# Values by key block with 128 columns of weights, and logits by blocks of 128 tokens, in a fused attention and mixture-of-experts kernel

## The chip, the core and the metric

The kernel runs on one core of a Trainium2 chip. The metric is the device time of one launch in microseconds. TensorE (PE in the profile) is the matmul engine; its weight loads are shown apart, as PEld. VectorE is DVE, ScalarE is ACT, GpSimd is POOL, and SyncE (SP) mostly issues DMAs.

## The reference

Eight batches with eight heads, 576 positions and 64 features a head, attend over a sliding window of 64 positions. Each of the 4608 tokens then goes to one of eight experts, the one with the highest logit.

```python
scores = scale * np.matmul(q, k.transpose(0, 1, 3, 2))
mask = (rel >= 0) & (rel < 64)                   # rel = query position - key position
attn = softmax(np.where(mask, scores, -1e9))
x = np.matmul(attn, v)                           # to rows of 512 = 8 heads x 64, one a token
logits = normalized(x) @ normalized(expert_emb).T / tau
e = argmax(logits)
out = gate * (relu(x @ w1[e]) @ w2[e])           # w1: 512 x 1024, w2: 1024 x 512
```

## The kernel before

**Tiling of the attention.** The tokens are cut into 36 blocks T of 128, each of two half blocks of 64: half z = 0 is key and query block 2T, half z = 1 is block 2T + 1. A batch has nine such 64-blocks, so batches begin at the 64-blocks 0, 9, 18 and so on; in eight of the 36 values of T one of the halves begins a batch and has no previous block. The window is as long as a 64-block, so a query sees its own block's keys up to itself and the previous block's keys behind that, 64 in all. The kernel keeps one score for each of the 64 places and notes by a mask which block it belongs to.

Heads lie in pairs: the partitions hold two heads hp of 64 features (or 64 keys) each, and u counts four such pairs. A matmul for one head, one half and one u therefore uses a 64x64 quarter of the 128x128 array, and four quarters (two hp, two z) can be at work at once. The profile writes this shape as 64\*64, rows by columns of the array that an instruction uses. A matmul of plain f32 operands that is written once in the program stands twice in the profile, as two weight loads and two matmuls; transposes and the experts' matmuls stand once.

**A step of the attention.** The loop `stages(s)` writes out one step for each block, a software pipeline over several blocks. In the order of PE's instructions:

- `scores(s)`, L215: 16 matmuls of 64\*64, 128 keys moving (64 where a batch begins)
- `logits(s - 4)`, L329: for each of four chunks c of 128 features and for each half of 64 tokens, a matmul with 64 columns of weights (the turned x, 128 features by 64 tokens) and 8 moving columns (the experts' embeddings), 128\*64 in the profile
- `attn_transposes(s - 1)`, L245, into `back`: four transposes of 128\*128
- `x_transposes(s - 3)`, L314, into `xback`: four transposes of 128\*128
- at times `ranks`, L366 and L367: two small bf16 matmuls
- `values(s - 2)`, L276: 32 matmuls of 64\*64 with 65 moving columns (64 features and a column of ones, for the softmax's sum), into the PSUM pair of banks `pair`

The other engines work beside it. ACT copies the own-block scores (L222), DVE puts the previous block's over them (`all_scores`, L225) and takes maxima (L229), POOL subtracts them (`less_max`, L233), ACT takes exponentials (L236). After the transposes ACT copies the turned weights into `aM[:, 0]` (L255); DVE writes `aM[:, 1]`, the weights times one mask (`attn_prev`, L258), and POOL multiplies `aM[:, 0]` by the other mask (`attn_own`, L261). DVE divides `pair` by the sums into rows of x (`x_out`, L297 to L299). POOL sends finished rows to their expert's place in DRAM by indirect DMAs (`place`, L412).

`values` takes the two masks in two passes. The first pass multiplies the weights that belong to the previous block (`aM[:, 1]`) with that block's values, the second those of the own block (`aM[:, 0]`, which POOL finishes last) with the own block's. Both pile up in `pair`. In each pass a half z meets another block of values, so z = 0 and z = 1 need matmuls of their own.

**After the loop.** The last blocks' steps are written out by hand and woven with the first expert slot's layer 1 (`layer1`, L827, fp32r operands, 128\*128, 256 moving columns). Then follow the counts and ranks of the tokens, the loads of the chosen experts' weights, and 20 slots of expert work (L827 and L887), which take the rest of the time.

Of the kernel before, what the change touches and what calls it, by code (L numbers as in the profile page):

```python
# [21 lines left out]
P = 128  # L22
B, H, S, D = 8, 8, 576, 64
N, DM, DF, E = 4608, 512, 1024, 8
WIN = 64
NB = S // WIN
# [29 lines left out]
K_ID, K_OWN, K_PREV, K_SEL, K_E, K_DESC, K_P, K_F, K_SL, K_U = 0, 128, 256, 384, 448, 456, 464, 465, 473, 476  # L56
# [3 lines left out]
def constants():  # L60
    c = np.zeros((P, K_W), np.float32)
    p = np.arange(P)
    c[:, K_ID:K_ID + P] = np.eye(P)

    r, col = (p % WIN)[:, None], (p % WIN)[None, :]
    c[:, K_OWN:K_OWN + P] = r <= col
    c[:, K_PREV:K_PREV + P] = r > col
    c[:, K_SEL:K_SEL + WIN] = col[:, :WIN] > r
    c[:, K_U:K_U + P] = p[:, None] < p[None, :]
    c[:, K_E:K_E + E] = np.arange(E) * N  # L70
    c[:, K_DESC:K_DESC + E] = E - np.arange(E)
    c[:, K_P] = p
    c[:, K_F:K_F + E] = (p[:, None] % 32) == np.arange(E)

    for a, (g, j) in POS.items():
        c[a, K_SL:K_SL + 3] = KIND[:g].count(KIND[g]), KIND[g] == "H", P * j
    t = np.full((P, NT + 1), OOB, np.int32)
    t[:, :NT] = np.arange(NT)[None, :] * P + p[:, None]
    return c, t
# [3 lines left out]
def attention_moe(ctx, tc, q, k, v, emb, tau, w1, w2, kc, kt, out):  # L83
    nc = tc.nc
# [46 lines left out]
    pair = psp.tile([P, 2, 512], F32, name="pair")  # L131
# [12 lines left out]
    embT = ap.tile([P, 4, 32], F32, name="embT", bufs=1)  # L144
# [37 lines left out]
    def vblock(g):  # L182
        return vb[:, g // 2 % RV, g % 2]

    sm, st = {}, {}
    sides = [(hp, z) for hp in range(2) for z in range(2)]
# [78 lines left out]
    def values(T):  # L265

        px[T] = pair
        m = aM.pop(T)
        o, p = m[:, 0], m[:, 1]
        for h, start in ((p, True), (o, False)):  # L270
            for u in range(4):
                for hp, z in sides:
                    g, pr, pz = 2 * T + z, slice(64 * hp, 64 * hp + 64), slice(64 * z, 64 * z + 64)
                    if start and g % NB == 0:
                        continue
                    nc.tensor.matmul(pair[pz, hp, u * (D + 1):(u + 1) * (D + 1)], lhsT=h[pr, u, pz],  # L276
                                     rhs=vblock(g - start)[pr, u], start=u == 0 and (start or g % NB == 0),
                                     stop=not start and u == 3)

    xr = {}  # L280
    NXR = 10
# [41 lines left out]
    def logits(T):  # L323
        G = OF[T]
        o2 = plv[:, G % 2, T - GROUPS[G][0]]
        t = xT.pop(T)
        for c in range(4):
            for o in (0, 64):
                nc.tensor.matmul(o2[o:o + 64], lhsT=t[:, c, o:o + 64], rhs=embT[:, c, :E],  # L329
                                 start=(c == 0), stop=(c == 3))  # L330

    def in_rows(G):

# [121 lines left out]
    for i, s0 in enumerate((8, 10, 15, 18, 21, 24, 26, 28)):  # L455
        c, h = divmod(i, 2)
# [3 lines left out]
    for i, s0 in enumerate((29, 30, 30, 31, 31, 32, 32, 33)):  # L460
        c, h = divmod(i, 2)
# [8 lines left out]
    def stages(s):  # L470
# [18 lines left out]
        if there(4):  # L489
            logits(s - 4)  # L490
# [12 lines left out]
        if there(2):  # L503
            values(s - 2)
# [176 lines left out]
    xb, xt, xp, ph, hp, po = {}, {}, {}, {}, {}, {}  # L681
# [344 lines left out]
    T, G = NT - 1, len(GROUPS) - 1  # L1026
# [16 lines left out]
    tokens(T - 2)  # L1043
    layer1(0, 0)
    logits(T - 4)
    own_scores(T)
    split_hi(0, w2raw, w2h)
# [5 lines left out]
    psm2 = ctx.enter_context(tc.tile_pool(name="psm2", bufs=1, space=PSUM, reuse_waits="tile"))  # L1053
    more = [psm2.tile([P, 512], F32, name=f"ph{i}") for i in (2, 3)]
    values(T - 2)
    maxima(T)
    xT_evac(T - 3)
# [8 lines left out]
    attn_halves(T - 1)  # L1066
    layer1(0, 2)
    logits(T - 3)
    ranks(G - 2)
    sum_counts(CUTS[1])  # L1070
# [11 lines left out]
    hidden_lo(0, 0)  # L1082
    x_transposes(T - 2, back)
    values(T - 1)
    xT_evac(T - 2)
    squares(T - 2)
# [112 lines left out]
def laid_out(inputs):  # L1199

    q, k, v = (np.asarray(inputs[n]).reshape(B, 4, 2, S, D) for n in "qkv")
    qt, kt = (x.transpose(2, 4, 1, 0, 3).reshape(P, 4, NT, P).transpose(2, 0, 1, 3).reshape(NT, P, 4 * P) for x in (q, k))
    vt = np.ones((2, WIN, B * NB, 4, D + 1), v.dtype)
    vt[..., :D] = v.reshape(B, 4, 2, NB, WIN, D).transpose(2, 4, 0, 3, 1, 5).reshape(2, WIN, B * NB, 4, D)
    vt = vt.reshape(P, NT, 2, 4, D + 1).transpose(1, 0, 2, 3, 4)

    col = np.arange(DM)
    feature = (col // D % 4 * 2 + col // (4 * D)) * D + col % D
    place = (col % P // 32) * P + col // P * 32 + col % 32
    c, t = constants()  # L1210
    given = {"q": qt, "k": kt, "v": vt, "emb": inputs["moe_expert_emb"][:, feature],
             "tau": np.reshape(inputs["moe_tau"], (1, 1)), "w1": inputs["moe_w1"][:, feature[place]],
             "w2": inputs["moe_w2"], "kc": c, "kt": t}
    return {n: np.ascontiguousarray(a) for n, a in given.items()}
# [16 lines left out]
```

## Time and profile before

| What | Value |
|---|---|
| time, median of 3 runs | 627.56 us (627.01 to 629.45) |
| the profiled execution: its own time | 626.38 us |
| its span, first to last instruction | 624.6 us |
| granted TensorE clock, mean | 0.994 |
| PE busy, of the span | 593.9 us, 95% |
| matmuls of `values` (L276) | 2176 in the profile |
| matmuls of `logits` (L329) | 576 in the profile |

The profile shows one execution. A row of a timeline has the start in us from the span's start, the time from the first start to the last end of the merged instructions, the engine, the line, the operation with its tiles (out<-in), the shape on the array, the size of the moving operand and the count. Matmuls are pipelined and their ends are modelled, so the distance from start to start tells more than the length of one.

### The profile page before, as it was taken

To read this page: it belongs to the slowest core of one execution; us is meant where nothing else is said; L and a number is where in the kernel's file an instruction comes from. 1 tells how busy PE (TensorE), PEld (TensorE's weight loads), DVE (VectorE), ACT (ScalarE), POOL (GpSimd) and SP (SyncE) were. 2 spreads that over 40 slices of the span, in tenths; PEclk is the share of its full clock that TensorE was granted. 3 is DMA by queue.
4 is the path that set the end of the run, shared out by engine and by line. 5 is a ranking of instruction groups with operands and counts; after the bars stand their busy time and mean duration, and the time that the engine had idled before them with its cause. 6 is when DMAs were issued, how large, how long until landed. Compare 5 with 4: busy or idle time off the path is not lost.

```text
span 624.6 us, 18570 instructions
## 1 busy us (share of the span) xinstructions
PE 593.9 (95%) x7210; PEld 531.1 (85%) x7210; DVE 426.0 (68%) x882; ACT 354.1 (57%) x559; POOL 241.6 (39%) x270
## 2 busy tenths in 40 slices
PE   8899989887898799999999999999999999999995
PEld 7787878776788699889988999899889998998884
DVE  2878888888677657676666776657666677657622
ACT  2666776766541346565466665646676476636533
POOL 2668888888732133213104431142023331222011
PEclk9999999999999999999999999999999999999998
DMA  8877888886334588877786897848788877775341
GB/s 302 266 218 252 272 257 268 268 252 196 143 111 184 134 274 259 267 216 253 234 277 212 284 315 221 277 161 305 241 265 236 285 264 213 238 275 195 116 163 37
DMA packets 85791, 143.79 MB, mean 230 GB/s; under 512 B 15797, under 2 KB 36021, under 8 KB 85696
## 3 DMA queue, kind: packets, MB, share of 16 engines
q1 hardware_dynamic: 74560, 112.87, 58.0%
q0 software_dynamic: 6000, 19.18, 7.8%
q10 hardware_dynamic: 5136, 10.49, 4.8%
q8 instruction: 58, 0.95, 0.6%
q14 instruction: 37, 0.30, 0.2%
HBM read 123.23 MB, written 20.05 MB: 229 GB/s over the span
## 4 chain that ended last, share of the span: by engine, by line
PE 71%; DVE 8%; POOL 7%; issue 7%; DMA 4%; ACT 2%; POOLq 0%; ACTq 0%; SPq 0%; DVEq 0%; another core or an unknown queue 0%
PE ph L827 31%; PE po L887 30%; PE pair L276 3%; PE ph L864 2%; POOL xs L412 2%; DMA kT<-in_k 2%; POOL sm L233 2%; POOL aM L261 2%; DMA w1raw<-in_w 1%; PE score L215 1%; PE back L245 1%; PE misc L329 1%; DVE sm L225 1%; ACT sm L236 1%; PE xback L314 1%
## 5 line engine op out<-in xcount | busy, mean ns | idle before, releaser
L827 PE MATMUL ph<-xh,w1l 128*128 128x256 f32 x576 | 161.4, 280 | 0.8 <-DVE w1l L161 0.8
L827 PE MATMUL ph<-xh,w1h 128*128 128x256 f32 x576 | 161.4, 280 | 0.0
L827 PE MATMUL ph<-xl,w1h 128*128 128x256 f32 x576 | 160.7, 279 | 0.0
L897 POOL DMA_INDIRECT out<-o,rest x39 | 50.5, 1295 | 221.4 <-ACT o L896 208.3
L887 PE MATMUL po<-w2l,hh 128*128 128x512 f32 x312 | 121.6, 390 | 2.4 <-DVE w2l L161 2.4
L887 PE MATMUL po<-w2h,hh 128*128 128x512 f32 x312 | 122.3, 392 | 0.0
L887 PE MATMUL po<-w2h,hl 128*128 128x512 f32 x312 | 121.9, 391 | 0.0
L841 DVE SCALAR_TENSOR_TENSOR hl<-ph,hh 128x512 fp32r<-128x512 f32 x78 | 53.4, 689 | 91.8 <-ACT hh L837 88.3
L161 DVE TENSOR_TENSOR w2l<-w2raw,w2h 128x1024 fp32r<-128x1024 f32 x80 | 94.8, 1221 | 24.5 <-ACT w2h L158 21.4
L827 PEld LDWEIGHTS ph<-xh,w1l 128*128 128x128 f32 x576 | 108.1, 188 | 1.2 <-DVE w1l L161 1.2
L827 PEld LDWEIGHTS ph<-xl,w1h 128*128 128x128 f32 x576 | 108.3, 188 | 0.8
L827 PEld LDWEIGHTS ph<-xh,w1h 128*128 128x128 f32 x576 | 107.7, 187 | 0.8
L158 ACT CAST w2h<-w2raw 128x1024 fp32r<-128x1024 f32 x80 | 81.5, 1048 | 39.9 <-PE po L887 30.4
L161 DVE TENSOR_TENSOR w1l<-w1raw,w1h 128x1024 fp32r<-128x1024 f32 x76 | 88.5, 1226 | 9.4 <-ACT w1h L158 9.1
L725 POOL TENSOR_TENSOR xl<-xt,xh 128x512 fp32r<-128x512 f32 x37 | 47.9, 1293 | 100.7 <-ACT xh L721 100.6
L837 ACT ACTIVATE hh<-ph 128x512 fp32r<-128x512 f32 x78 | 46.1, 596 | 55.1 <-PE ph L827 44.1
L158 ACT CAST w1h<-w1raw 128x1024 fp32r<-128x1024 f32 x76 | 73.9, 1047 | 0.0
L887 PEld LDWEIGHTS po<-w2l,hh 128*128 128x128 f32 x312 | 58.6, 188 | 14.4 <-DVE w2l L161 2.8
L887 PEld LDWEIGHTS po<-w2h,hl 128*128 128x128 f32 x312 | 58.6, 188 | 12.7
L887 PEld LDWEIGHTS po<-w2h,hh 128*128 128x128 f32 x312 | 58.6, 188 | 11.5
L721 ACT CAST xh<-xt 128x512 fp32r<-128x512 f32 x39 | 24.1, 620 | 62.5 <-DVE xt L710 60.3
L276 PE MATMUL pair<-v,aM 64*64 64x65 f32 x2176 | 51.4, 226 | 8.5 <-issue 7.4
(180 smaller groups left out, 828.6 us busy)
## 6 DMA issues: line engine op xcount, KB each, us to landing
w2raw<-in_w SPq DMA_DIRECT2D x76, 512.0 KB
w1raw<-in_w SPq DMA_DIRECT2D x72, 512.0 KB
xb<-xs SPq DMA_DIRECT2D x156, 64.0 KB
v<-in_v SPq DMA_DIRECT2D x36, 260.0 KB
qT<-in_q SPq DMA_DIRECT2D x36, 256.0 KB
kT<-in_k ACTq DMA_DIRECT2D x32, 256.0 KB
w1raw<-in_w SPq DMA_DIRECT2D x8, 256.0 KB
w2raw<-in_w SPq DMA_DIRECT2D x8, 256.0 KB
```

The costliest lines, as they stand in the source:

```text
L158: nc.scalar.copy(hi[c], raw[c])
L161: eng.tensor_tensor(out=lo[c], in0=raw[c], in1=hi[c].bitcast(F32), op=ALU.subtract)
L233: nc.gpsimd.tensor_tensor(out=t, in0=t, in1=st.pop(T).unsqueeze(2).to_broadcast([P, 8, WIN]), op=ALU.subtract)
L261: nc.gpsimd.tensor_tensor(out=aM[T][:, 0], in0=aM[T][:, 0], in1=halves[:, 0].unsqueeze(1).to_broadcast([P, 4, P]), op=ALU.mult)
L276: nc.tensor.matmul(pair[pz, hp, u * (D + 1):(u + 1) * (D + 1)], lhsT=h[pr, u, pz], rhs=vblock(g - start)[pr, u], start=u == 0 and (start o ...
L721: nc.scalar.copy(xh, t)
L725: eng.tensor_tensor(out=xl, in0=t, in1=xh.bitcast(F32), op=ALU.subtract)
L827: nc.tensor.matmul(o, lhsT=ww[c][:, f * P:(f + 1) * P], rhs=xx[:, c, :n], start=(c == 0 and i == 0), stop=(c == 3 and i == 2))
L837: nc.scalar.activation(hh, ph[g, part], AF.Relu)
L841: nc.vector.scalar_tensor_tensor(out=hl, in0=ph.pop((g, part)), scalar=0.0, in1=hh.bitcast(F32), op0=ALU.max, op1=ALU.subtract)
L887: nc.tensor.matmul(po[a], lhsT=xx[:, f, at], rhs=ww[f // 2][:, f % 2], start=(f == 0 and i == 0), stop=(f == 7 and i == 2))
L897: d = nc.gpsimd.indirect_dma_start(out=out, out_offset=bass.IndirectOffsetOnAxis(ap=tok, axis=0), in_=o, in_offset=None, bounds_check=N - ...
```

## The change

The masks are cut by key block and not by own and previous. `aM[:, 0]` ("mine") now holds all weights that go with the values of 64-block 2T: the own weights of half z = 0 and the previous-block weights of half z = 1. `aM[:, 1]` ("other") holds the rest: the previous weights of z = 0, which go with block 2T - 1, and the own weights of z = 1, which go with block 2T + 1. The engines that write them do the same work as before, with other constants.

"Mine" is then one block of values for both halves, so one matmul a head takes all 128 queries as its columns of weights: 64 rows by 128 columns. "Other" stays with 64\*64 matmuls. Where a half begins a batch, "mine" is split into halves again, or covers z = 0 alone. `logits` drops its loop over the two halves of 64 tokens and takes 128 columns of weights.

```diff
-    c[:, K_OWN:K_OWN + P] = r <= col
-    c[:, K_PREV:K_PREV + P] = r > col
+    here = (r <= col) == (p < WIN)[None, :]
+    c[:, K_OWN:K_OWN + P] = here
+    c[:, K_PREV:K_PREV + P] = ~here
...
-        o, p = m[:, 0], m[:, 1]
-        for h, start in ((p, True), (o, False)):
-            for u in range(4):
-                for hp, z in sides:
-                    g, pr, pz = 2 * T + z, slice(64 * hp, 64 * hp + 64), slice(64 * z, 64 * z + 64)
-                    if start and g % NB == 0:
-                        continue
-                    nc.tensor.matmul(pair[pz, hp, u * (D + 1):(u + 1) * (D + 1)], lhsT=h[pr, u, pz],
-                                     rhs=vblock(g - start)[pr, u], start=u == 0 and (start or g % NB == 0),
-                                     stop=not start and u == 3)
+        mine, other = m[:, 0], m[:, 1]
+        g = 2 * T
+        first = [(g + z) % NB == 0 for z in range(2)]
+        for u in range(4):
+            for hp, z in sides:
+                if z == 0 and first[0]:
+                    continue
+                pr, pz = slice(64 * hp, 64 * hp + 64), slice(64 * z, 64 * z + 64)
+                nc.tensor.matmul(pair[pz, hp, u * (D + 1):(u + 1) * (D + 1)], lhsT=other[pr, u, pz],
+                                 rhs=vblock(g - 1 + 2 * z)[pr, u], start=u == 0, stop=first[z] and u == 3)
+        rows = [slice(0, P)] if not any(first) else [slice(0, 64)] if first[1] else [slice(0, 64), slice(64, P)]
+        for u in range(4):
+            for hp in range(2):
+                pr = slice(64 * hp, 64 * hp + 64)
+                for pz in rows:
+                    nc.tensor.matmul(pair[pz, hp, u * (D + 1):(u + 1) * (D + 1)], lhsT=mine[pr, u, pz],
+                                     rhs=vblock(g)[pr, u], start=u == 0 and first[0] and pz.start == 0, stop=u == 3)
...
-            for o in (0, 64):
-                nc.tensor.matmul(o2[o:o + 64], lhsT=t[:, c, o:o + 64], rhs=embT[:, c, :E],
-                                 start=(c == 0), stop=(c == 3))
+            nc.tensor.matmul(o2, lhsT=t[:, c], rhs=embT[:, c, :E], start=(c == 0), stop=(c == 3))
```

Only PE's instructions change. A row below has the line, the operation, its tiles and the size of what it writes, partitions by columns; "x32" is a run of 32 alike. This is PE before, from the values of one regular block through the next step to the values of a block where a batch begins:

```order
L276 MATMUL pair<-v,aM 64x65 x32
L215 MATMUL score<-kT,qT 64x128 x16
L329 MATMUL misc<-embT,xT 64x8 x8
L245 MATMUL back<-cs,sm 128x128 x4
L314 MATMUL xback<-cs,xr 128x128 x4
L276 MATMUL pair<-v,aM 64x65 x24
```

And this is PE in the changed kernel at the same place (L278 is "other", L285 is "mine", L216, L336, L246 and L322 are the scores, logits and the two transposes):

```order
L278 MATMUL pair<-v,aM 64x65 x16
L285 MATMUL pair<-v,aM 128x65 x8
L216 MATMUL score<-kT,qT 64x128 x16
L336 MATMUL misc<-embT,xT 128x8 x4
L246 MATMUL back<-cs,sm 128x128 x4
L322 MATMUL xback<-cs,xr 128x128 x4
L278 MATMUL pair<-v,aM 64x65 x16
L285 MATMUL pair<-v,aM 64x65 x8
```

A regular block's 32 matmuls became 16 of the old shape and 8 that write all 128 partitions; the block where a batch begins keeps 24 of the old shape; the logits' 8 became 4. Nothing moved past anything else. In the profile, where each of these counts twice, L276's 2176 become 1728 (28 regular blocks of 48, eight of 48) and L329's 576 become 288.

## The prediction

> **What bounds the kernel now.** I read the page first, then the busy times of the engines by stage, then PE's groups and its timeline in the attention. The page gives the span and PE's share; the stages (start and end, length, then the busy time of each engine, its clock, the DMA share and GB/s) show where the change lies.
>
> ```profile
> span 624.6 us, 18570 instructions
> PE 593.9 (95%) x7210; PEld 531.1 (85%) x7210; DVE 426.0 (68%) x882; ACT 354.1 (57%) x559; POOL 241.6 (39%) x270
> ...
> 24.70:154.30 129.60, 117.62 (x3581) 103.20 (x3583) 108.97 (x253) 89.38 (x197) 105.39 (x143) 1.00 0.79 245
> 154.30:192.00 37.70, 32.57 (x553) 28.92 (x554) 27.71 (x100) 16.62 (x32) 20.22 (x29) 0.95 0.38 128
> ```
>
> The first stage holds 30 blocks of the attention, 4.32 us each. PE is the busiest engine (117.62 of 129.60), with DVE (108.97) and POOL (105.39) close. The clock is full, so the throttle is no part of this. What each of PE's groups does there, and what PE waited for:
>
> ```profile
> L276 PE MATMUL pair<-v,aM 64*64 64x65 f32 x1808 | 41.7, 223 | 6.3 <-issue 5.8
> L329 PE MATMUL misc<-embT,xT 128*64 128x8 f32 x482 | 19.4, 205 | 0.9 <-DVE embT L451 0.8
> ...
> PE pair L276 <- issue: 5.8, 13, 1.3
> PE score L215 <- issue: 2.4, 4, 0.9
> PE score L215 <- DVE sm L225: 1.6, 1, 1.6
> PE back L245 <- ACT sm L236: 1.3, 2, 0.9
> ```
>
> 1808 = 23 x 64 + 7 x 48: 23 regular blocks and seven where a batch begins. 482 is 30 logits. To see what a block costs when nothing disturbs it, here is a step from logits to logits in PE's timeline, and three rows of its loads:
>
> ```profile
> 28.21 0.64 PE L329 MATMUL misc<-embT,xT 128*64 128x8 f32 x16
> 28.78 0.66 PE L245 MATMUL back<-cs,sm 128*128 128x128 f32 x4
> 29.27 0.60 PE L314 MATMUL xback<-cs,xr 128*128 128x128 f32 x4
> 29.80 1.16 PE L276 MATMUL pair<-v,aM 64*64 64x65 f32 x64
> 30.78 1.05 PE L215 MATMUL score<-kT,qT 64*64 64x128 f32 x32
> 31.77 0.64 PE L329 MATMUL misc<-embT,xT 128*64 128x8 f32 x16
> ...
> 28.21 0.55 PEld L329 LDWEIGHTS misc<-embT,xT 128*64 128x64 f32 x16 [0.17 <-issue]
> 29.16 0.47 PEld L314 LDWEIGHTS xback<-cs,xr 128*128 128x128 f32 x4
> 29.80 1.02 PEld L276 LDWEIGHTS pair<-v,aM 64*64 64x64 f32 x64 [0.17 <-issue]
> ```
>
> The step takes 31.77 - 28.21 = 3.56 us, so 30 of them are 106.8, and 129.6 - 106.8 = 22.8 us of the stage are something else: the waits above (11.9 with the 0.8 for embT), and small stops, rank matmuls and beginnings of batches (10.9). The "issue" stops fall within runs of matmuls that have no wait:
>
> ```profile
> 128.57 1.08 PE L276 MATMUL pair<-v,aM 64*64 64x65 f32 x57
> 130.05 0.34 PE L276 MATMUL pair<-v,aM 64*64 64x65 f32 x7 [0.40 <-issue]
> ...
> q8 instruction: 58, 0.95, 0.6%
> ```
>
> The queue brought 0.95 MB in 58 packets, 16.4 KB each, while PE ran 2 x 7210 loads and matmuls: 249 for a packet. I take these stops for PE running out of fetched instructions. Fewer instructions should bring fewer of them. That is the change's best hope.
>
> **How PE's time is made up: rounds.** In `values` four quarters work at once. 64 loads are 16 rounds of four; they span 1.02 us and one lasts 0.13 (row below), so a round takes (1.02 - 0.13) / 15 = 0.059 us. In the logits two halves work at once: eight rounds in (0.55 - 0.14) / 7 = 0.059. Both have 64 columns of weights, but one moves 65 columns and the other eight. So the load sets the round, not the moving side; moving 128 columns does take longer, (1.05 - 0.27) / 7 = 0.111 for L215 (one lasts 0.27). What do 128 columns of weights cost? Loads by form, name, shape, count, busy, mean ns:
>
> ```profile
> L276 PEld LDWEIGHTS pair<-v,aM 64*64 64x64 f32 x1808 | 34.9, 133 | 13.0 <-issue 12.7
> L329 PEld LDWEIGHTS misc<-embT,xT 128*64 128x64 f32 x484 | 16.7, 137 | 6.0 <-issue 3.4 <-DVE embT L451 1.1 <-ACT sm L236 0.7
> L245 PEld LDWEIGHTS back<-cs,sm 128*128 128x128 f32 x120 | 12.6, 140 | 2.9 <-ACT sm L236 2.1
> ...
> L827 PEld LDWEIGHTS ph<-xl,w1h 128*128 128x128 f32 x576 | 108.3, 188 | 0.8
> ...
> 22.36 0.32 PEld L450 LDWEIGHTS xback<-cs,xr 8*128 8x128 f32 x4 [0.81 <-ACT xT L318]
> ...
> 163.08 0.28 PE L827 MATMUL ph<-xh,w1l 128*128 128x256 f32 x1
> 163.29 0.64 PE L329 MATMUL misc<-embT,xT 128*64 128x8 f32 x16
> 163.86 0.39 PE L827 MATMUL ph<-xh,w1h 128*128 128x256 f32 x1
> 164.08 0.28 PE L827 MATMUL ph<-xl,w1h 128*128 128x256 f32 x1
> 164.20 0.28 PE L827 MATMUL ph<-xh,w1l 128*128 128x256 f32 x1
> ```
>
> No plain f32 matmul with 128 columns of weights is in the trace, so it has two bounds. Low: the transposes of L450, 128 columns with eight moving, follow each other at (0.32 - 0.14) / 3 = 0.060. High: L827's matmuls follow at 0.12 (164.08 to 164.20). The lengths of the loads decide between them: 133 for 64 columns and 188 for 128 is 55 ns more for 64 columns more, which is the 0.059 round again, while a transpose's 140 for 128 columns stands apart. The new matmuls multiply and don't transpose, so I take the high side, and of it 0.11, twice 0.055. L827's first matmul behind the logits agrees: it needs 0.22 to the next instead of 0.12, so 0.10 of load lay bare.
>
> [...]
>
> **A change of shape on the array.** From the last L827 at 163.08 the next of its kind was due at 163.20; the logits came at 163.29, 0.09 later. From the last transpose (29.27 + 3 x 0.11 = 29.60, due 29.71) to the values at 29.80 it is 0.09 again, from the last score round (30.78 + 7 x 0.111 = 31.56, due 31.67) to the logits 0.10. So a change of shape costs 0.10 and lays the first load bare: 0.05 for 64 columns, 0.10 for 128, 0.06 for a transpose (0.66 against 0.60). That 64\*64 to 64\*128 costs it too isn't in the trace; it lies between 0 and 0.20, and I take the same 0.10.
>
> [...]
>
> **The change part by part.**
>
> - Masks: other constants, the same instructions on DVE, ACT and POOL. Nothing. No wait is added: POOL's `aM[:, 0]` is still read by the second half of `values`.
> - `values`, regular block: now 16 x 0.059 = 0.94. After: "other" is 32 loads on four quarters, eight rounds of 0.059 = 0.47; a change of shape, 0.10 + 0.10; "mine" is 16 loads on two row halves, eight rounds of 0.11 = 0.88; and a change back to the scores, 0.10 + 0.05. Sum 1.70, **0.76 more**. The number of rounds stays at 16; what the change saves are matmuls that ran at the same time as others.
> - `values` where a batch begins: the same shapes and count. 0.
> - Logits: now 0.05 bare, 8 x 0.059 = 0.47, change to the transposes 0.10 + 0.06: 0.68. After: 0.10 bare, 8 x 0.11 = 0.88, no change behind: 0.98, **0.30 more**. `x_out` waits for `values` on DVE; the next scores on PE hide that.
> - Instructions of a block: 16 + 8 + 32 matmuls of four instructions and eight transposes of two are 240; after, 16 + 4 + 24 give 192. A fifth fewer packets.
>
> The stage: 23 x 0.76 + 30 x 0.30 = 17.5 + 9.0 = 26.5 us more for PE. Of the 22.8 us that aren't clean steps some are given back. The waits for others (3.7) go, since PE comes later. Of the 8.2 of "issue" I keep 3.3: a fifth fewer packets, and PE takes longer over each. Of the other 10.9 I keep half, 5.5. So 106.8 + 26.5 + 8.8 = 142.1, **12.5 more** than 129.6. The bounds: all 22.8 given back, +3.7; nothing, +26.5.
>
> In the second stage I read the chain that ended last, and PE's groups there:
>
> ```profile
> 160.50 1.20 PE score L215 x31
> ...
> 185.13 2.04 PE ph L827 x12
> ...
> L276 PE MATMUL pair<-v,aM 64*64 64x65 f32 x256 | 6.9, 244 | 1.6 <-issue 1.6
> L329 PE MATMUL misc<-embT,xT 128*64 128x8 f32 x96 | 3.8, 205 | 0.1
> ```
>
> From 160.50 to 185.13 + 2.04 = 187.17 the chain runs on PE almost without a break, so delays there move the loads of the experts' weights behind them. Four regular blocks cost 4 x 0.76 = 3.0. Six logits stand between L827's: the gap from 163.20 to 163.96 is 0.76 now, and would be 0.88 + 0.10 without changes, 0.22 more, 1.3 in all. Of the stops, 1.6, I give back half, 0.8: **+3.5**. Ahead of 24.7 lies one regular block, T = 1, among waits for loads: 0 to 0.76, I take 0.3. From 192 on nothing changes.
>
> Sum 12.5 + 3.5 + 0.3 = 16.3. The profiled execution took 626.38 us, so 642.7; the median of the runs, 627.56, is 0.2% above it. I forecast **643 us**.
>
> **The rivals.**
>
> - A, fast loads: a plain f32 load of 128 columns takes L450's 0.060. Then a regular block is 0.47 + 0.16 + 0.48 + 0.15 = 1.26, 0.32 more, and the logits are 0.06 + 0.48 = 0.54, 0.14 less. The stage: 23 x 0.32 - 30 x 0.14 = +3.2 on PE, and of the 22.8 more comes back than that: with two thirds of the "issue" stops (5.5) and a fifth of the other 10.9 (2.2) it is -4.5, so 622 us (618 to 628). For it: f32 and 128 columns, as in L450. Against: L450 transposes, and the two plain lengths of 133 and 188. This is the way to a faster kernel, and it turns where a round r, which costs the stage 23 x (9r - 0.22) + 30 x (9r - 0.68) = 477r - 25.5, makes up for the 7.7 that come back: at r = 0.070.
> - B, no overlap of the row halves: the 16 loads of "mine" stand one after another. Eight rounds more of 0.11 in 27 blocks, +24: 667 us, slower still. Against: four quarters do overlap in L276, two of them being row halves.
> - C, PE has the room: DVE or POOL bound the steps and hide 1 us of PE each: 626 to 630. Against: the step's 3.56 plus 1.06 is more than the 4.32 that it takes now, and PE has only 12.0 us idle.
>
> **How the numbers follow.** Forecast 0.75, its own range 632 to 657 from the bounds of what is given back (+3.7 and half of the end's 3.5, or +26.5 and 4.3). A 0.15, B 0.05, C 0.05. The range of 624 to 652 leaves out B, most of A's and the top of the forecast's: a fifth. Within 0.5%, or 3.1 us, no difference can be told. Faster: 0.12, A without its upper end. Same: 0.03 of A and 0.04 of C and 0.01 of the forecast, 0.08. Slower: the rest, 0.80.
>
> **What would show it.** Right: loads of L285 and L336 near 188 ns, sixteen of L285 in about 1 us and eight of L336 in 0.95, 0.2 between L278's last matmul and L285's first, steps of about 4.7 us. Wrong: loads near 138, eight of L336 in half a us, and "issue" all but gone with steps under 4.3.

## The result and the profile after

The changed kernel took 1.0092 times the time of the kernel before, 95% interval 1.0064 to 1.012: 0.9% slower, some 5.8 us. The forecast was slower by 2.5%. (The plain medians, 639.10 us against 629.62, say more because the ratio leaves out slow runs at a lower granted clock, six of the changed kernel's 20.) The profiled execution took 634.32 us with a span of 632.5, 7.9 more than the span before.

First the page and the stages of the profile after, with the columns as before. The second row of stages begins with the 31st logits, as the second row ahead of the prediction (154.30:192.00) does for the kernel before.

```profile
span 632.5 us, 17094 instructions
PE 614.7 (97%) x6474; PEld 555.0 (88%) x6474; DVE 426.1 (67%) x882; ACT 356.2 (56%) x559; POOL 241.7 (38%) x270
...
q8 instruction: 53, 0.87, 0.6%
```

```profile
24.70:154.30 129.60, 129.12 (x2795) 117.09 (x2792) 102.50 (x242) 86.25 (x185) 100.03 (x133) 0.99 0.78 237
...
162.20:199.90 37.70, 35.37 (x450) 32.89 (x447) 29.60 (x106) 16.63 (x32) 21.15 (x29) 0.95 0.34 115
```

PE was busy for 117.62 us of the first 129.60 before; now it is for 129.12. Behind its first wait of 0.5 us it never stands still. Here is all that PE waited for in that stage, and one regular step in its timeline with the loads of its new matmuls:

```profile
PE misc L336 <- DVE embT L457: 0.5, 1, 0.5
```

```profile
54.06 1.06 PE L336 MATMUL misc<-embT,xT 128*128 128x8 f32 x8
54.97 0.64 PE L246 MATMUL back<-cs,sm 128*128 128x128 f32 x4
55.44 0.60 PE L322 MATMUL xback<-cs,xr 128*128 128x128 f32 x4
55.97 0.70 PE L278 MATMUL pair<-v,aM 64*64 64x65 f32 x32
56.60 1.11 PE L285 MATMUL pair<-v,aM 64*128 64x65 f32 x16
57.64 1.10 PE L216 MATMUL score<-kT,qT 64*64 64x128 f32 x32
58.67 0.72 PE L336 MATMUL misc<-embT,xT 128*128 128x8 f32 x5
```

```profile
L336 PEld LDWEIGHTS misc<-embT,xT 128*128 128x128 f32 x232 | 28.1, 191 | 5.3 <-issue 2.9 <-ACT sm L237 1.0 <-DVE embT L457 0.7
L285 PEld LDWEIGHTS pair<-v,aM 64*128 64x128 f32 x352 | 21.6, 189 | 1.6
...
51.98 0.97 PEld L285 LDWEIGHTS pair<-v,aM 64*128 64x128 f32 x16
54.06 0.97 PEld L336 LDWEIGHTS misc<-embT,xT 128*128 128x128 f32 x8 [0.17 <-issue]
```

The step takes 58.67 - 54.06 = 4.61 us; the forecast for it was 3.56 + 1.06 = 4.62. The loads last 189 and 191 ns, their rounds (0.97 - 0.19) / 7 = 0.111 us. So PE's price was right to a hundredth, and the error lies elsewhere. Three stretches show where the 7.9 us come from. Before, the first logits start at 24.65 and the 31st at 154.22; after, at 25.38 and 162.18:

```profile
24.65 0.64 PE L329 MATMUL misc<-embT,xT 128*64 128x8 f32 x16 [0.84 <-DVE embT L451]
...
154.22 0.64 PE L329 MATMUL misc<-embT,xT 128*64 128x8 f32 x16
...
25.38 1.06 PE L336 MATMUL misc<-embT,xT 128*128 128x8 f32 x8 [0.48 <-DVE embT L457]
...
162.18 1.06 PE L336 MATMUL misc<-embT,xT 128*128 128x8 f32 x8
```

| Stretch | Before | After | More | Forecast |
|---|---|---|---|---|
| to the first logits | 24.65 | 25.38 | 0.7 | 0.3 |
| 30 steps | 129.6 | 136.8 | 7.2 | 12.5 |
| from the 31st logits to the end | 470.4 | 470.3 | -0.1 | 3.5 |

### The profile page after: what moved, and what is told of

It reads as the page before. It is cut to its first block, busy times and chain, and to the rows that moved or that the text cites. A ratio compares the mean times of both kernels' runs of the same rounds, so it can differ in the third digit from the quotient of the medians.

```text
span 632.5 us, 17094 instructions
## 1 busy us (share of the span) xinstructions
PE 614.7 (97%) x6474; PEld 555.0 (88%) x6474; DVE 426.1 (67%) x882; ACT 356.2 (56%) x559; POOL 241.7 (38%) x270
## 4 chain that ended last, share of the span: by engine, by line
PE 84%; DVE 5%; issue 4%; DMA 2%; POOL 2%; ACT 1%; POOLq 0%; ACTq 0%; another core or an unknown queue 0%; DVEq 0%
PE ph L833 31%; PE po L893 30%; PE misc L336 5%; PE pair L285 4%; PE score L216 4%; PE pair L278 3%; PE back L246 2%; PE ph L870 2%; PE xback L322 2%; DMA w1raw<-in_w 2%; PE back L474 1%; DVE w1l L162 1%; DMA out<-o,rest 1%; POOL xs L418 1%; POOL sm L234 1%
## 5 line engine op out<-in xcount | busy, mean ns | idle before, releaser
L234 POOL TENSOR_TENSOR sm<-sm,st 128x512 f32<-128x512 f32 x36 | 37.4, 1040 | 35.0 <-DVE st L230 31.6
```

What stands on the lines that cost most here:

```text
L234: nc.gpsimd.tensor_tensor(out=t, in0=t, in1=st.pop(T).unsqueeze(2).to_broadcast([P, 8, WIN]), op=ALU.subtract)
```

## The experiments

Nine kernels ran, all timed in five rounds against the kernel before. The question was why PE's 26.5 us more cost so little. The first theory (S) was that PE's stops for instructions had been eaten up; P and W were its rivals. S speaks of packets of 256 instructions: the trace of before has packets of 16384 bytes, and stops 256 instructions apart (below). That 128 of them are what has to last is an assumption; in that trace the packets start 53 to 221 instructions ahead.

**The logits alone.** In `logits` the edit is that of the change, the rest is the kernel before.

```diff
-            for o in (0, 64):
-                nc.tensor.matmul(o2[o:o + 64], lhsT=t[:, c, o:o + 64], rhs=embT[:, c, :E],
-                                 start=(c == 0), stop=(c == 3))
+            nc.tensor.matmul(o2, lhsT=t[:, c], rhs=embT[:, c, :E], start=(c == 0), stop=(c == 3))
```

> Only the logits take 128 columns of weights; the values stay as before. Theory S (stops): a step of the kernel before has 3.56 us of matmuls and some 0.7 us in which PE stands, mostly for its next 256 instructions, because 128 instructions go by faster than a packet of 256 arrives; slower rounds and fewer instructions eat into that before they cost time. The logits add 0.30 us a step and drop the instructions from 240 to 224, so the step grows by 0.05 to 0.1 us only and the time by 1 to 3 us: ratio to before 1.002 to 1.005. Theory P (proportion): each part costs its share of PE's added time, 9.0 of 26.5, of the 5.8 us measured: 2.0 us, 1.003. The two differ in the stops: under S PE's issue stops in the stage of the attention fall below half of the 8.2 us of before, under P they stay near 8.

Measured: 0.9974, 0.9947 to 1.0002. Neither theory had it so low. PE's issue stops in the stage:

```profile
PE pair L276 <- issue: 4.6, 5, 1.8
...
PE score L215 <- issue: 0.7, 1, 0.7
```

5.3 us in place of 8.2: less, but not below half.

**The values alone.** The changed kernel with the logits of before.

> Only the values are cut by key block, with 64*128 matmuls; the logits stay in two halves. Theory S: the step has 3.56 + 0.76 = 4.32 us of matmuls in a regular block, 208 instructions, hardly a stop left; regular steps of about 4.35 and the rest near 4.0 give 0 to 1.5 us over before: ratio 1.000 to 1.003. Theory P: 17.5 of 26.5 of the 5.8 us: 3.8 us, 1.006. Under S this and the logits alone add up to clearly less than the whole change's 1.009; under P to the same.

Measured: 0.9961, 0.9925 to 0.9996. The stops are down to 1.5 us, in a profile (635.66 us) whose PE ran at half the clock from 24.27 to 44.74:

```profile
PE score L216 <- issue: 0.8, 1, 0.8
PE pair L285 <- issue: 0.7, 1, 0.7
```

P falls: the parts give about -0.3% and -0.4%, and the whole +0.9%. There is room for one part, and not for both. S had the sense of it, and both sizes a little high.

**More work for PE, with more instructions.** Behind the transposes of x:

```diff
+            for _ in range(10):
+                nc.tensor.matmul(misc[:, 256:], lhsT=ones, rhs=low, start=True, stop=True)
```

> The kernel before, with ten bf16 matmuls of 256 moving columns added in each step behind the transposes of x; their results go to spare columns that nobody reads. They make PE busy for some 1.1 us a step more, as the change does, but with 20 instructions more (260) in place of 48 fewer (192). Theory S: the run of 128 instructions in the values still goes by in under 1 us, so the stops stay: steps of 3.56 + 1.1 + 0.2 to 0.4 = 4.9 to 5.1 us, the attention 17 to 22 us longer, ratio 1.025 to 1.035. Rival W (waits): what PE lost in its steps before was slack that any busier PE takes up, and the number of instructions has no part in it: steps of 4.65 to 4.75 us, 10 to 12 us more, ratio 1.015 to 1.02, and no issue stops.

Measured: 1.0189, 1.0164 to 1.0214, with 1.8 us of issue stops.

```profile
PE misc L329 <- issue: 0.9, 1, 0.9
PE score L215 <- issue: 0.6, 1, 0.6
...
PE pair L276 <- issue: 0.3, 1, 0.3
```

That is W's range, and S in this form fell: the quick run of 128 in the values was untouched, and the stops were all but gone all the same.

**The two passes of the values apart.**

```diff
...
         scores(s)
+        if there(2):
+            values(s - 2, (True,))
...
-            values(s - 2)
+            values(s - 2, (False,))
```

> The kernel before with the two passes of the values apart: the first pass right behind the scores of the next step, the second where both were. The same instructions; the run of 128 quick ones is cut into two of 64 with the logits and the transposes between. Theory S: the stop of a packet depends on how fast its 128 neighbours go by; the quickest 128 now take about 1.5 us and not 0.95, so the long stops shrink and the step falls by 0.1 to 0.25 us unless PE waits for the division of the values before: 3 to 7 us less, ratio 0.989 to 0.995. Rival W: nothing but the order moves, 0.998 to 1.004.

Measured: 1.0022, 1.0001 to 1.0043. What PE waited for:

```profile
PE pair L278 <- DVE xr L301: 11.2, 20, 0.9
PE pair L278 <- DVE xmore L301: 3.5, 7, 0.6
PE score L215 <- issue: 1.1, 2, 0.6
...
PE back L245 <- issue: 0.4, 1, 0.4
PE pair L278 <- issue: 0.3, 1, 0.3
```

The stops went to 1.8 us, as S had it, but the first pass waits for DVE's division of the last values out of `pair`, 14.7 us. S had named that condition; W's time is right, with another content. The run settles nothing between them.

**A new theory, K.** Most stops don't come at any instruction. The loads start again in the kernel before at 38.64 and 42.83, and from one restart to the next PE has 127 matmuls, 127 loads and two semaphore instructions, which the views don't count, 256:

```profile
38.64 0.37 PEld L276 LDWEIGHTS pair<-v,aM 64*64 64x64 f32 x18 [0.35 <-issue]
42.83 0.26 PEld L276 LDWEIGHTS pair<-v,aM 64*64 64x64 f32 x11 [0.30 <-issue]
...
38.63:42.82 4.19, 4.03 (x127) 3.49 (x127) 3.88 (x12) 2.86 (x8) 2.92 (x6) 1.00 0.72 212
42.82:47.82 5.00, 4.00 (x127) 3.55 (x127) 4.07 (x8) 2.99 (x8) 3.30 (x6) 1.00 0.68 220
```

Counted so, 12 of the 17 stops of the stage, 6.8 of the 8.2 us, stand an exact multiple of 256 from each other; the other five stay unexplained. In the first eight of the nine kernels run here all 53 stops do; the ninth has none. In the trace of DMA packets of the kernel before, q8 brings one for every 249 of PE's recorded loads and matmuls (58 for 14420). PE passes no such place less than 2.2 us after a packet's start, and in the 12 stops it goes on 2.2 to 2.9 us after one.

The packets of the stage start 53 to 221 instructions ahead of the place, 137 on the mean, so K takes what counts to be how long half a packet, 128 instructions, lasts: under some 2.3 us PE must stop for the next, well above it not.

K's half packet is 128 times a clean step over its instructions: before 128 x 3.56 / 240 = 1.90 us; the logits alone 128 x 3.86 / 224 = 2.21; with the ten matmuls 128 x 4.66 / 260 = 2.29; the values alone 128 x 4.32 / 208 = 2.66; the whole change 128 x 4.62 / 192 = 3.08. The stops were 8.2, 5.3, 1.8, 1.5 and 0 us: they fall with it, and at 2.66 they aren't gone. That the packet comes with a fixed lead of half isn't shown: in the changed kernel the packets start 182 instructions or more ahead. K and W still give the same for most of these, since PE's work rose in all of them. The next two runs add the same PE time with many instructions and with few.

**Sixteen small matmuls, and four long ones.**

```diff
+            for _ in range(16):
+                nc.tensor.matmul(misc[:, 256:256 + 8], lhsT=ones, rhs=low[:, :8], start=True, stop=True)
```

> The kernel before with sixteen bf16 matmuls of eight moving columns added behind the transposes of x in each step, results in spare columns that nobody reads: 32 instructions more (272 a step) that take PE only some 0.45 us. Theory K (pace): PE's instructions come in packets of 256, the next one is asked for about half a packet ahead and is there some 2.3 us later. A packet then takes no less than its own half at PE's speed and 2.3 us, whatever else happens. The clean step is 4.01 us, half a packet 1.9, a packet 4.2, a step 4.2 x 272/256 = 4.45, with ranks and beginnings 4.55 to 4.65: 7 to 10 us over before, ratio 1.011 to 1.016, and issue stops of 8 us or more. Theory W (waits): the number of instructions has no part; 4.01 is still under the 4.3 that a step takes, so 0 to 1.5 us, ratio up to 1.003.

```diff
+            for _ in range(4):
+                nc.tensor.matmul(misc[:, 256:256 + 256], lhsT=ones, rhs=low[:, :256], start=True, stop=True)
```

> The same PE time as the sixteen small matmuls, about 0.45 us a step, from four bf16 matmuls of 256 moving columns: eight instructions more (248). Theory K: half a packet lasts 2.07 us, a packet 4.37, a step 4.37 x 248/256 = 4.23, with ranks and beginnings 4.3 to 4.4: 0 to 3 us over before, ratio 1.000 to 1.005, and clearly under the sixteen small ones. Theory W: the same as the sixteen small ones, ratio up to 1.003.

Measured: the small ones 1.0192, 1.0137 to 1.0247; the long ones 1.0031, 0.9999 to 1.0064. PE's stops, first with the small ones, then with the long:

```profile
PE score L215 <- issue: 3.9, 4, 1.6
PE pair L276 <- issue: 3.9, 5, 2.5
PE back L245 <- issue: 2.2, 1, 2.2
PE misc L329 <- issue: 1.4, 2, 0.9
PE misc L500 <- issue: 1.1, 2, 0.6
```

```profile
PE pair L276 <- issue: 3.1, 6, 0.9
PE score L215 <- issue: 2.6, 4, 1.2
...
PE misc L329 <- issue: 0.7, 2, 0.5
```

12.5 us against 6.4. W is out: 24 instructions a step more, at nearly the same PE time (3.94 - 3.56 = 0.38 us for the small ones, 0.44 for the long, from 64.62 to 65.06 in their run) and under what a step takes anyway, cost 1.6%. K's figure for the small ones was even too low. Part of the cost is the clock: behind their three longest stops (2.24, 1.58 and 2.55 us) PE ran at half the clock for 3.4 us each, from 101.77, 112.00 and 152.97, and the steps there took 5.3 to 8.3 us, where one without stops takes 3.94; with the long ones the stage has no such stretch. K doesn't explain the two longest: ahead of the 2.24 and the 2.55 the packet itself started only when PE had come to the place. Why it came so late stays open.

**The first pass behind the logits.** As with the passes apart, but the first pass stands behind `logits(s - 4)`.

> The kernel before with the first pass of the values behind the logits of the next step, where the division of the last values is done by then; one change of shape more a step (0.15 us), 240 instructions as before. Theory K: half a packet lasts 1.98 us, a packet 4.28, a step 4.0 and with ranks and beginnings 4.1 to 4.2, no wait of the first pass: 3 to 5 us less than before, ratio 0.992 to 0.996. Theory W: the order changes nothing, and 0.15 us are taken up: 0.999 to 1.003. Both would be wrong if the division still comes late: then waits of the first pass on DVE of 5 us or more.

Measured: 0.9969, 0.9933 to 1.0005. The stops are 4.7 us and the wait for the division 2.4. The middle lies just above K's range and the interval reaches into W's too, so the time settles nothing; the stops came back where the wait went, as K has it.

**The price of a change of shape.** The two masks change places between the buffers, so that DVE's, which is ready early, is "mine"; "mine" comes first and "other" stands beside the scores of its own shape.

```diff
-    c[:, K_OWN:K_OWN + P] = here
-    c[:, K_PREV:K_PREV + P] = ~here
+    c[:, K_OWN:K_OWN + P] = ~here
+    c[:, K_PREV:K_PREV + P] = here
...
-        mine, other = m[:, 0], m[:, 1]
+        other, mine = m[:, 0], m[:, 1]
...
```

With the logits in halves:

> The values by key block with the logits in halves (as in the run of the values alone), but the masks are swapped between the two buffers so that the 64*128 half of the work comes first and the 64*64 half stands next to the scores of the same shape. One change of shape and one bare load less in a regular step: behind the transposes 0.09 + 0.10, between the two halves 0.10 + 0.05, none before the scores, 0.34 in place of 0.49. Theory C (each change of shape is paid on PE): 0.15 us less in 28 steps, 4.2 us, as long as PE is the bound: from the 0.996 of the values alone to 0.989 to 0.991. Rival O (other engines): without its stops PE at 4.15 a step is under what DVE, POOL and their waits need, some 4.2 to 4.3: 0.993 to 0.997, with PE waits of several us.

With the whole change:

> The whole change, the 64*128 half first as in the run beside it. PE bounds every step of the changed kernel (4.62 us, no wait), so here the 0.15 us must show whole: steps of 4.47, 4.2 us less in all than the changed kernel, ratio to before 1.002 to 1.004. If a change of shape costs nothing where the loads already set the pace, the ratio stays at 1.008 to 1.010.

Measured: with the whole change 1.0062, 1.0021 to 1.0104; with the logits in halves 1.0012, 0.9978 to 1.0046. A regular step of the latter, and one of the values alone, from logits to logits:

```profile
85.42 0.64 PE L337 MATMUL misc<-embT,xT 128*64 128x8 f32 x16
87.02 1.11 PE L278 MATMUL pair<-v,aM 64*128 64x65 f32 x16
88.06 0.70 PE L285 MATMUL pair<-v,aM 64*64 64x65 f32 x32
88.58 1.05 PE L216 MATMUL score<-kT,qT 64*64 64x128 f32 x32
89.56 0.64 PE L337 MATMUL misc<-embT,xT 128*64 128x8 f32 x16
```

```profile
98.79 0.64 PE L337 MATMUL misc<-embT,xT 128*64 128x8 f32 x16
100.38 0.70 PE L278 MATMUL pair<-v,aM 64*64 64x65 f32 x32
101.01 1.11 PE L285 MATMUL pair<-v,aM 64*128 64x65 f32 x16
102.05 1.10 PE L216 MATMUL score<-kT,qT 64*64 64x128 f32 x32
103.08 0.64 PE L337 MATMUL misc<-embT,xT 128*64 128x8 f32 x16
```

4.14 us in place of 4.29: the 0.15 of a change of shape shows whole in the step. From "other" to the scores it is 0.52 (88.06 to 88.58), 0.05 over its eight rounds of 0.059; from "mine" to the scores it is 1.04, 0.15 over its eight of 0.111. With the whole change the step is 4.46 (85.59 to 90.05) in place of 4.62. The time doesn't follow. With the whole change it lies between the two ranges, and the interval reaches into both. With the halves it is 1.001 and not 0.990, and the interval overlaps that of the values alone; O's range ends at 0.997, just below the interval, so both theories miss there. Of PE's waits in that run 3.0 us are for ACT's exponentials and 2.7 are stops, which isn't enough to say what else fills the steps; that stays open. Of the nine kernels only the values alone have an interval below 1, and that by a hair.

## Why the prediction was wrong

- **The load of 128 columns: right.** 0.11 us a round was forecast, 0.111 measured, with loads of 189 and 191 ns. The lengths of the loads told it (133 for 64 columns, 188 for 128), not the nearest row by shape, the transposes of L450. Rivals A and B fall with it: the sixteen loads of "mine" take 0.97 us.
- **The change of shape: right,** 0.15 us with its bare load in the mine-first runs. 64\*64 to 64\*128 had no row, and the step with it came out at 4.61 against 4.62.
- **The sum of PE's work: right.** 23 steps of 4.62 and seven of 3.86 are 133.3 us, and the 30 steps took 136.8.
- **What is given back: wrong,** and this is the step that failed: "Of the 8.2 of "issue" I keep 3.3: a fifth fewer packets, and PE takes longer over each. Of the other 10.9 I keep half, 5.5." Of 8.8 us kept there were 3.5, and some 1.5 of those are new: the first step took 31.53 - 25.38 = 6.15 us, 1.5 over a clean one, at half the clock (below). I let the stops shrink with the number of packets and PE's pace. The runs show that they vanish: in the changed kernel each packet of the stage starts at least 4.1 us before PE comes to the place, where the 12 stops of before ended 2.2 to 2.9 us after one, and PE never stops. The trace of before held what was needed: stops 256 instructions apart.
- The 10.9 were misread too. PE's idle time understates a stop, since the modelled ends of the last matmuls reach into it: the row of 130.05 has 0.40 idle, and from the start before it (129.43) it is 0.62. From start to start the kernel before has, beside the wait for DVE, 24 breaks of over 0.2 us within its values and scores, 14.1 us in all, where a round takes 0.06 to 0.11. So some 12 of the 22.8 us were such breaks. At full clock the changed kernel has none, apart from the 0.20 at its changes of shape and one wait for DVE. The forecast's own lower bound, +3.7, was nearer to the 7.2 than its 12.5.
- **The end: wrong,** +3.5 forecast, -0.1 measured. The 37.7 us from the 31st logits on hold 35.37 of PE's work, 2.8 more than the 32.57 before, and the rest of the program took no longer. I let PE's chain set the end from 160.50 on, and gave back only half the stops; PE's idle time there fell from 5.1 to 2.3 us and took the work in. This rests on one profile of each kernel, and in the profiles of the nine other kernels this stretch lasts 465 to 473 us, so a term of 3.5 is hardly told from chance here.
- **The direction and the size:** 16.3 us forecast, 7.9 in the profiled execution, 5.8 by the ratio of the runs. Of the 26.5 us more of PE's work the 30 steps took in 19.3, and some 12 of that fit into PE's own stops. Rival C named the right thing, room on PE, with the wrong owner and size: not DVE or POOL hid PE's work, for the most part, but PE's own stops had left room.

Stops for instructions cost time here: the kernel before has 12 in the stage that stand multiples of 256 instructions apart, 6.8 us, and 24 instructions more a step at nearly the same PE time cost 1.6%, part of it by the clock.

## What to carry to other kernels

In these traces plain f32 matmuls with 8 or 65 moving columns took 0.059 us a round with 64 columns of weights and 0.111 with 128, so joining two 64-column matmuls that already ran side by side saved no PE time and added changes of shape (0.15 us each with the bare load). Divide PE's time for a step without stops by its instructions before pricing an edit there. In the stage of these kernels PE stopped for 4.7 to 12.5 us where that gave 14 to 17 ns, for 1.5 to 2.7 us from 18 to 21 ns, and not at all from 23 on; slower or fewer instructions were free as long as there were stops to take them in (the logits alone 0.9974, the values alone 0.9961). Look for such slack by the distance of unexplained stops in instructions, and by starts rather than by idle time; two edits that each fit into it may not fit together.

## What the runs showed of the hardware

The stops for instructions weren't expected to vanish. They can be long: with the sixteen small matmuls a single one lasted 2.24 us, between two transposes:

```profile
98.20 0.44 PE L245 MATMUL back<-cs,sm 128*128 128x128 f32 x2
100.87 0.38 PE L245 MATMUL back<-cs,sm 128*128 128x128 f32 x2 [2.24 <-issue]
```

The granted clock fell to half for 3.4 us in the changed kernel's first full step, with PE busy all the time:

```profile
26.30:29.70 3.40, 3.40 (x46) 2.95 (x47) 1.45 (x3) 2.03 (x5) 2.39 (x3) 0.50 0.56 169
```

The kernel before has no such stretch there, but one at 155.84. In the values alone it lasted from 24.27 to 44.74, in the whole change with "mine" first from 25.34 to 42.41. In the first 235 us of the eleven profiles PE stood for 0.9 to 2.9 us of the 3.4 us (the length of this stretch) ahead of each stretch at half the clock: 1.0 ahead of this one, 2.2, 1.6 and 2.5 ahead of those of the small ones. But PE stood for 1.7 of the 3.4 us from 186.60 in the kernel before, and the clock behind them was full, so these traces don't give the rule.

Logits' loads of 128 columns aren't needed for such a stretch: with the first pass behind the logits, where those loads have 64 columns, the clock was half from 25.86 to 32.69.
